# Retention and two MLPs on one core: two PSUM rings and a new order in the head, weight loads in quarters, and S3·T3 ahead of S1·T1 in the MLP pairs

## The chip, the cores and the metric

The kernel runs on one core of one Trainium2 chip. The metric is the time of one execution on the device in microseconds (us), lower is better. The kernel before takes 574.09 us, the median of three runs (573.87 to 574.21).

## The reference

Retention (a linear attention with decay) over 2 batches, 8 heads, 768 positions and head size 64, and then two MLPs on the 1536 tokens that it gives. The first MLP squares a ReLU, the second takes a leaky ReLU. q, k, v are float32, the weights are float64 and are converted on the chip.

```python
def _attn_ref(q, k, v, lam):
    Dmask = np.where(rel >= 0, lam[:, None, None] ** rel[None, :, :], 0.0)
    for b in range(nb):                      # blocks of positions
        intra = np.einsum('bhic,bhjc->bhij', qb, kb) * Dmask[None]
        intra = np.einsum('bhij,bhjd->bhid', intra, vb)
        inter = np.einsum('bhid,bhde->bhie', qb * lam_pow[None], kv_state)
        out[:, :, sl] = intra + inter
        kb_dec = kb * rev_pow[None]
        kv_state = lam_block[None, :, None, None] * kv_state + np.einsum('bhsd,bhse->bhde', kb_dec, vb)

def _moe_ref(x, w_in, w_out):                # x: 1536 x 512, d_ff 2048
    h = np.maximum(x @ w_in, 0.0)
    return (h * h @ w_out).astype(np.float32)

def _moe2_ref(x, w_in, w_out):
    h = x @ w_in
    g = np.maximum(0.01 * h, h)
    return (g @ w_out).astype(np.float32)
```

## The kernel before

**Precision.** Each operand of the MLPs is kept as a high and a low part (names with h and l), split by a cast on ACT and a subtraction on DVE (`split`, L68 to L70). A product is three matmuls: high by high, high by low, low by high. `three` (L523) issues them all from L525.

**Retention (the head).** The work goes in 12 units, i = 0 to 11: two batches of six chunks of 128 positions. For a unit, T(i) (`transposes`, L279) turns k and q on TensorE and ACT copies them out as kT and qT (L283); `scores` (L296) multiplies them into two PSUM banks; `mask` (L301, DVE) multiplies the scores by the decay table `DTr` into Pm; `state` takes k scaled by the decay (kd, L314, POOL), multiplies it with v (L320) and has DVE add the old state to it (`st`, L332, or L334 in the first chunk of a batch); the last chunk of a batch has no state. `output` (L345, L347) adds the state's part and Pm times v, and `split` makes xhi and xlo of the result. Every PSUM tile comes from one pool of eight banks in turn (`bank`, L59), the filler of `warm` included, and a tile takes its bank when the readers of the tile eight places before are done. `warm(n)` issues n transposes of the identity that nobody reads.

**Loads.** SP issues all loads in the order of the program: k and q four units ahead, v two units ahead, 256 KB each. Weights come in pieces of 1 MB (`fetch`, L92): two halves of the first MLP's first 512 columns, at i = 1 and i = 9, and the next behind retention. `converting` (L100) turns a piece from float64 into float32 in steps: on ACT `Abs` (L111), on DVE L112, L113, L115 and L118, then a cast to the high part on ACT (L132) and the low part on DVE (L134). During retention one step is placed in each of the units 3 to 7 (`convert(pin=True)`).

**The MLPs.** Each has four stages (l, s) of 512 columns of d_ff, and three token tiles of 512. From stage (0,1) on, tiles 0 and 1 are taken together in `first_pair`, a Strassen-like scheme of seven products in place of eight: A11·B11, S2·T2, A22·T4, S1·T1, S3·T3, A12·B21 and S4·B22, each for the halves h = 0, 1 of the columns. S1 to S4 are sums of weight blocks (`weight_sums`, L418; tiles `sw`, made by L423 to L426, a cast L427 and a subtraction L428), T1 to T4 sums of token blocks. PSUM tile A takes the A products, B takes S2·T2 and S3·T3, C takes S1·T1 and S4·B22, D takes A22·T4. `plus` (L595, DVE) adds them up, and `put` sends the finished block m = 2h + i of token tile t to `activate`: in layer 0 a ReLU, and its square twice, on ACT (L461 to L463), and the low part `g0l` or `g1l` on DVE (L467). Then `second(l, s, 0)` multiplies the blocks m = 0 to 3 of tile 0, in this order, by the second weight.

**What sets the order.** SP and TensorE run in the order of the program, in retention and, for TensorE, in the MLPs (`manual_schedule`). On ACT, DVE and POOL a scheduler sets the order at build time, by priorities: steps that are pinned (`keep_in_program_order`) keep their place, and `high_priority(offset=400)` in `put` and `plus` moves work forward. Each engine then runs its list in that order.

## Time and profile before

| what | before |
|---|---|
| median of three runs | 574.09 us (573.87 to 574.21) |
| the profiled execution's own time | 573.56 us |
| its span, first to last instruction | 571.6 us |
| TensorE (PE) busy | 561.2 us, 98% of the span |
| VectorE (DVE), ScalarE (ACT), GpSimd (POOL) busy | 71%, 53%, 16% |
| mean granted TensorE clock | 0.996 |
| first MLP matmul | 63.10 us from the span's start |

The profile is of one execution. Its page has the busy time of each engine, and views of the trace show single instructions in order of time, who waited for whom, the DMA issues with their time to landing, and the busy time in stretches that one chooses. The start of an instruction that had to wait carries the idle time ahead of it and what released it.

### The profile page before, as it was taken

How to read it: one execution, taken by the hardware profiler on the slowest of the kernel's cores; microseconds unless marked ns; L12 is line 12 of the kernel's file. 1: busy time of each engine (PE TensorE's matmuls, PEld its weight loads, DVE VectorE, ACT ScalarE, POOL GpSimd, SP SyncE). 2: the span in 40 equal slices, each digit the busy share in tenths (PEclk: the TensorE clock that was granted, in tenths of full speed). 3: DMA queues.
4: the chain of work that ended last, by engine and by line, in shares of the span. 5: the costliest groups of instructions: out<-in, count | busy, mean ns of one | idle time of the engine just before them, and what ended most of it. 6: DMA issues, size and time to landing. Idle time of an engine off the chain costs nothing.

```text
span 571.6 us, 8193 instructions
## 1 busy us (share of the span) xinstructions
PE 561.2 (98%) x3159; PEld 472.7 (83%) x3159; DVE 407.6 (71%) x595; ACT 304.6 (53%) x486; POOL 89.3 (16%) x101
## 2 busy tenths in 40 slices
PE   7999999999999999999999999999999999999997
PEld 7889888888788878888788888888888888888897
DVE  3588899999745584819888996719663492718887
ACT  2344589553974457733948555543662284435610
POOL 3659100000023202130000000000203101220032
PEclk9999999999999999999999999999999999999999
DMA  8998544535157744294413324354429505560444
GB/s 172 246 209 183 191 147 148 186 146 188 71 73 185 110 148 73 67 202 127 163 32 104 120 73 148 110 185 130 66 43 226 126 4 71 60 87 1 145 151 148
DMA packets 68472, 72.37 MB, mean 127 GB/s; under 512 B 39753, under 2 KB 43857, under 8 KB 68433
## 3 DMA queue, kind: packets, MB, share of 16 engines
...
q10 hardware_dynamic: 672, 0.39, 0.3%
q8 instruction: 25, 0.41, 0.3%
...
## 4 chain that ended last, share of the span: by engine, by line
PE 75%; DVE 11%; ACT 6%; DMA 4%; issue 2%; POOL 0%; SPq 0%; ACTq 0%; DVEq 0%; POOLq 0%
PE ps L525 67%; DMA raw<-in_moe_w_in 3%; DVE hb L118 2%; PE ps L279 2%; ACT f L461 2%; PE ps L296 2%; DMA raw<-in_moe_w_out 2%; PE ps L347 1%; DVE hb L115 1%; DVE f L595 1%; ACT g0h L462 1%; PE ps L345 1%; ACT hb L111 1%; ACT f L463 1%; PE ps L320 1%
## 5 line engine op out<-in xcount | busy, mean ns | idle before, releaser
L644 POOL DMA_DIRECT2D spill<-f x48 | 42.7, 918 | 408.3 <-ACT f L640 408.3
L525 PE MATMUL ps<-xhi,w1h 128*128 128x512 f32 x216 | 84.1, 390 | 0.0
L525 PE MATMUL ps<-xhi,w1l 128*128 128x512 f32 x216 | 84.0, 389 | 0.0
L525 PE MATMUL ps<-xlo,w1h 128*128 128x512 f32 x216 | 84.0, 389 | 0.0
L640 ACT COPY f<-ps 128x512 f32<-128x512 f32 x72 | 41.7, 584 | 70.3 <-PE ps L525 69.8
L134 DVE TENSOR_TENSOR w2l<-hb,w2h 128x1024 fp32r<-128x1024 f32 x16 | 19.6, 1227 | 61.1 <-ACT w2h L132 60.7
L467 DVE TENSOR_TENSOR g0l<-f,g0h 128x512 fp32r<-128x512 f32 x52 | 34.7, 686 | 34.2 <-ACT f L463 18.3
L595 DVE TENSOR_TENSOR f<-ps,f 128x512 f32<-128x512 f32 x70 | 45.7, 684 | 9.8 <-PE ps L525 9.3
L525 PEld LDWEIGHTS ps<-xhi,w1h 128*128 128x128 f32 x216 | 40.5, 188 | 8.5 <-issue 0.2
L525 PEld LDWEIGHTS ps<-xhi,w1l 128*128 128x128 f32 x216 | 40.5, 188 | 8.4
L525 PEld LDWEIGHTS ps<-xlo,w1h 128*128 128x128 f32 x216 | 40.5, 188 | 8.4
L525 PE MATMUL ps<-g0l,w2h 128*128 128x512 f32 x112 | 43.9, 392 | 3.0 <-DVE g0l L467 3.0
L111 ACT ACTIVATE hb<-raw 128x1024 f32<-128x1024 f32 x32 | 36.8, 1149 | 14.4 <-DMA raw<-in_moe_w_in 8.7
L118 DVE SCALAR_TENSOR_TENSOR hb<-raw,hb 128x1024 uint16<-128x1024 uint32 x32 | 43.6, 1364 | 0.4
L525 PE MATMUL ps<-g0h,w2l 128*128 128x512 f32 x112 | 43.6, 389 | 0.0
L525 PE MATMUL ps<-g0h,w2h 128*128 128x512 f32 x112 | 43.6, 389 | 0.0
L525 PE MATMUL ps<-t,sw 128*128 128x512 f32 x168 | 40.4, 389 | 0.0
L525 PE MATMUL ps<-w2l,g0h 128*128 128x512 f32 (+1 forms) x104 | 39.6, 381 | 0.0
L525 PE MATMUL ps<-w2h,g0l 128*128 128x512 f32 (+1 forms) x104 | 39.6, 381 | 0.0
L525 PE MATMUL ps<-w2h,g0h 128*128 128x512 f32 (+1 forms) x104 | 39.6, 381 | 0.0
L115 DVE SCALAR_TENSOR_TENSOR hb<-raw,hb 128x1024 uint32<-128x1024 uint32 x32 | 39.1, 1221 | 0.4
L525 PEld LDWEIGHTS ps<-t,sw 128*128 128x128 f32 x168 | 31.5, 188 | 6.5
...
## 6 DMA issues: line engine op xcount, KB each, us to landing
...
spill<-f POOLq DMA_DIRECT2D x48, 256.0 KB, 4.6
spill<-f SPq DMA_DIRECT2D x24, 256.0 KB, 3.1
k<-in_k SPq DMA_DIRECT2D x12, 256.0 KB, 4.7
q<-in_q SPq DMA_DIRECT2D x12, 256.0 KB, 5.0
v<-in_v SPq DMA_DIRECT2D x12, 256.0 KB, 5.3
f<-spill SPq DMA_DIRECT2D x12, 256.0 KB, 2.6
```

The costliest lines, as they stand in the source:

```text
L111: nc.scalar.activation(hf, w_hi.bitcast(F32), AF.Abs)
L115: yield ve.scalar_tensor_tensor(out=hb, in0=w_hi, scalar=0xC0000000, in1=hb, op0=ALU.bitwise_and, op1=ALU.bitwise_or)
L118: step = ve.scalar_tensor_tensor(out=half, in0=w_lo, scalar=2.0 ** -29, in1=half, op0=ALU.mult, op1=ALU.add)
L134: yield ve.tensor_tensor(out=lo, in0=hf, in1=hi, op=ALU.subtract)
L279: nc.tensor.transpose(ps[:, p, :], src[:, 2 * p:2 * p + 2, :].rearrange("s h d -> s (h d)"), ident)
L296: nc.tensor.matmul(raw_scores[i][par][:, p, :], kT[i][r, p, :], qT[i][r, p, :], start=True, stop=True)
L461: nc.scalar.activation(r, src, AF.Relu)
L467: nc.vector.tensor_tensor(out=glo, in0=r, in1=ghi, op=ALU.subtract)
L525: nc.tensor.matmul(ps, a, b, start=start and n == 0, stop=stop and n == len(ops) - 1, skip_group_check=again)
L595: ve.tensor_tensor(out=out, in0=ps[h, where], in1=other, op=ALU.add)
L640: nc.scalar.copy(f, src)
L644: nc.gpsimd.dma_start(dst, f, accum_op=ALU.add)
```

## The change

It has three parts. Line numbers shift by 7 in retention (L296 becomes L303), by 8 in `converting` (L111 becomes L119) and by 16 in the MLPs (L428 becomes L444, L467 becomes L483, L595 becomes L611).

1. **Head.** During retention PSUM is a pool of two rings of four banks: scores in one, everything else in the other. Behind `state(0)` come nine filler transposes, and T(2) stands ahead of `mask(0)` and `output(0)`. T(3) and `state(2)` stand behind `output(1)`, where T(3) stood ahead of it and `state(2)` behind T(4). For the MLPs a pool of eight banks in one ring is opened.
2. **Weights.** `fetch_by_rows` issues the two halves of the first weight as four loads of 256 KB each, one at each of the units 1 to 8; at i = 9 the first piece of the second weight follows. The conversion steps stand at the units 6 to 11. Later fetches hang on the conversion of the piece before.
3. **Pairs.** In `first_pair`, S3·T3 with its sums and the block m = 2h + 1 of tile 0 stands ahead of S1·T1. The sums per half are as many as before: r22 = B + s1, s1 = D + r22, and r22 + C once C is there.

```diff
@@ -54,10 +54,10 @@
     raw = ctx.enter_context(tc.tile_pool(name="raw", bufs=2))
     fp = ctx.enter_context(tc.tile_pool(name="fp", bufs=9))
     cv = ctx.enter_context(tc.tile_pool(name="cv", bufs=1))
-    psum = ctx.enter_context(tc.tile_pool(name="psum", bufs=8, space=bass.MemoryType.PSUM))
-
-    def bank():
-        return psum.tile([P, 512], F32, tag="ps", name="ps")
+    banks = []
+
+    def bank(tag="ps"):
+        return banks[-1].tile([P, 512], F32, tag=tag, name="ps")
 
     def plain():
         return fp.tile([P, TT], F32, tag="f", name="f")
@@ -89,6 +89,14 @@
     fetched, at_work = [], []
     wts, sums, opened = {}, {}, set()
 
+    def fetch_by_rows():
+        key = todo.pop(0)
+        r = raw.tile([P, 4 * CW], I64, tag="raw", name="raw")
+        fetched.append((key, r))
+        for k in range(4):
+            dma(r.rearrange("p (k f) -> p k f", k=4)[:, k], source(*key)[:, k])
+            yield
+
     def fetch():
         if todo:
             key = todo.pop(0)
@@ -116,7 +124,7 @@
                                       op0=ALU.bitwise_and, op1=ALU.bitwise_or)
 
         step = ve.scalar_tensor_tensor(out=half, in0=w_lo, scalar=2.0 ** -29, in1=half, op0=ALU.mult, op1=ALU.add)
-        if begun_mlp:
+        if key != order[0]:
             fetch()
         yield step
         if (l, s) != stages[0] and n == 0:
@@ -156,7 +164,6 @@
                 tc.keep_in_program_order(step)
 
 
-    begun_mlp = []
     opened.update(order[:5])
 
     xhi = [None] * NTILE
@@ -167,6 +174,7 @@
         xlo[t] = xp.tile([P, KD, TT], F32R, tag=f"xlo{t}", name=f"xlo{t}")
 
     def retention(ctx_att, att):
+        banks.append(ctx_att.enter_context(tc.tile_pool(name="early", bufs=4, space=bass.MemoryType.PSUM)))
         nat = {
             name: ctx_att.enter_context(tc.tile_pool(name="nat" + name, bufs=n))
             for name, n in (("k", 5), ("q", 3), ("v", 3))
@@ -198,9 +206,8 @@
         make_identity(nc, ident)
 
 
-        idle = bank()
-
         def warm(n):
+            idle = bank()
             for _ in range(n):
                 tc.keep_in_program_order(nc.tensor.transpose(idle[:, 0:P], ident, ident))
 
@@ -289,7 +296,7 @@
                 nc.gpsimd.tensor_tensor(out=qS[i], in0=qT[i], in1=LR, op=ALU.mult)
 
         def scores(i):
-            raw_scores[i] = [bank().rearrange("p (a s) -> p a s", a=NP) for _ in range(2)]
+            raw_scores[i] = [bank("scores").rearrange("p (a s) -> p a s", a=NP) for _ in range(2)]
             for p in range(NP):
                 for par in range(2):
                     r = slice(par * D, (par + 1) * D)
@@ -367,30 +374,38 @@
         scale_q(1, q1)
         scores(1)
         state(0)
+        warm(9)
+        q2 = transposes(2)
         mask(0)
         output(0)
-        scale_q(2, transposes(2))
+        scale_q(2, q2)
         state(1)
         mask(1)
         scores(2)
+        pieces = chain(fetch_by_rows(), fetch_by_rows())
         for i in range(n_units):
-            if i and i + 2 < n_units:
+            if i > 1 and i + 2 < n_units:
                 scale_q(i + 2, transposes(i + 2))
             if i + 4 < n_units:
                 load(i + 4, "kq")
             if i + 2 < n_units:
                 load(i + 2, "v")
-            if i in (1, 9):
+            if 1 <= i <= 8:
+                next(pieces)
+            if i == 9:
                 fetch()
             if i:
-                if i > 1:
+                if i > 2:
                     state(i)
                 output(i)
+                if i == 1:
+                    scale_q(3, transposes(3))
+                    state(2)
                 if i + 1 < n_units:
                     mask(i + 1)
                 if i + 2 < n_units:
                     scores(i + 2)
-            if 3 <= i <= 7:
+            if 6 <= i:
                 convert(pin=True)
 
 
@@ -398,7 +413,8 @@
         att = ctx_att.enter_context(tc.tile_pool(name="att", bufs=1))
         with tc.manual_schedule(engines={mybir.EngineType.SP, mybir.EngineType.PE}):
             retention(ctx_att, att)
-
+    banks.append(ctx.enter_context(
+        tc.tile_pool(name="psum", bufs=8, space=bass.MemoryType.PSUM, reuse_waits="tile")))
 
     late = ctx.enter_context(tc.tile_pool(name="late", bufs=1, reuse_waits="tile"))
     spill = [[[dram.tile([P, DM], F32, name=f"spill{l}{t}{m}") for m in range(4)] for t in range(NTILE)]
@@ -611,18 +627,18 @@
         if last:
             opened.add(("sums", l, s))
         for h in both:
+            product(h, "B", "S3", "T3", False)
+            r22[h] = plain()
+            plus(h, r22[h], "B", s1[h])
+            plus(h, s1[h], "D", r22[h])
+            put(h, s1[h], s1[h], 1, 0)
+            yield last
+        for h in both:
             product(h, "C", "S1", "T1")
+            plus(h, r22[h], "C", r22[h])
             yield True
         for h in both:
-            product(h, "B", "S3", "T3", False)
-            plus(h, s1[h], "B", s1[h])
-            r22[h] = plain()
-            plus(h, r22[h], "C", s1[h])
-            plus(h, s1[h], "D", s1[h])
-            yield last
-        for h in both:
             put(h, product(h, "A", "A12", "B21", False), plain(), 0, 0)
-            put(h, s1[h], s1[h], 1, 0)
             yield last
         for h in both:
             product(h, "C", "S4", "B22", False)
@@ -792,8 +808,6 @@
             return parts + [first(l, s, 2)] + [second_last(s, t) for t in range(NTILE)]
         return parts + [second(l, s, 0), first(l, s, 2), second(l, s, 1), second(l, s, 2)]
 
-    begun_mlp.append(True)
-    fetch()
     opened.update(order[:7])
     with tc.manual_schedule(engines={mybir.EngineType.PE}):
         for l, s in stages:
```

How the compiled order of the instructions changes is shown at three places, on the engines whose order the scheduler sets; TensorE's and SP's order is that of the code above. A row is a line of the program, the operation, the tile written and the tiles read.

**DVE, in stage (0,1), from the conversion of a weight piece to the sums of the pair.** `hb_1663` (after, `hb_1678`) is the piece, L595 (L611) the `plus` sums. Before:

```order
L113 TENSOR_SCALAR hb_1663<-hb_1663 128x1024
L115 SCALAR_TENSOR_TENSOR hb_1663<-raw_1562,hb_1663 128x1024
L118 SCALAR_TENSOR_TENSOR hb_1663<-raw_1562,hb_1663 128x1024
L595 TENSOR_TENSOR f_1608<-ps_1623,f_1608 128x512
L595 TENSOR_TENSOR f_1689<-ps_1666,f_1608 128x512
L595 TENSOR_TENSOR f_1618<-ps_1636,f_1618 128x512
```

After:

```order
L121 TENSOR_SCALAR hb_1678<-hb_1678 128x1024
L611 TENSOR_TENSOR f_1695<-ps_1649,f_1631 128x512
L123 SCALAR_TENSOR_TENSOR hb_1678<-raw_1577,hb_1678 128x1024
L611 TENSOR_TENSOR f_1631<-ps_1671,f_1695 128x512
L611 TENSOR_TENSOR f_1708<-ps_1660,f_1643 128x512
L611 TENSOR_TENSOR f_1695<-ps_1715,f_1695 128x512
```

Both of the piece's long steps stood ahead of the six sums. Now the first of them (L123) stands between the sum r22 = B + s1 of half 0 and the sum s1 = D + r22 made from it, and the second comes after the sums.

**DVE, in stage (0,1), ahead of `second(l, s, 0)`.** `g0l` are the low parts of tile 0's blocks, L428 (after, L444) is the subtraction for `sw`. Before:

```order
L467 TENSOR_TENSOR g0l_1598<-f_1608,g0h_1597 128x512
L595 TENSOR_TENSOR f_1630<-ps_1666,f_1630 128x512
L595 TENSOR_TENSOR f_1643<-ps_1674,f_1643 128x512
L467 TENSOR_TENSOR g0l_1598<-f_1723,g0h_1597 128x512
L467 TENSOR_TENSOR g0l_1598<-f_1618,g0h_1597 128x512
L428 TENSOR_TENSOR sw_1633<-rb_1632,sw_1633 128x1024
```

After:

```order
L483 TENSOR_TENSOR g0l_1621<-f_1643,g0h_1620 128x512
L611 TENSOR_TENSOR f_1656<-ps_1715,f_1656 128x512
L483 TENSOR_TENSOR g0l_1621<-f_1741,g0h_1620 128x512
L611 TENSOR_TENSOR f_1667<-ps_1724,f_1667 128x512
L444 TENSOR_TENSOR sw_1646<-rb_1645,sw_1646 128x1024
L483 TENSOR_TENSOR g0l_1621<-f_1752,g0h_1620 128x512
```

The third block's low part, `g0l_1598<-f_1723` before and `g0l_1621<-f_1752` after, stood ahead of the subtraction for `sw` and right behind the two last sums. Now the last sum and the subtraction stand in front of it.

**ACT, at the end of retention.** L283 (after, L290) are the copies kT and qT, L69 the high part of an output, L111 (L119) a conversion's `Abs`, L140 the cast of a converted piece; the two rows `xhi2` in each list are those of units 9 and 10. Before:

```order
L283 COPY kT_865<-ps_860 128x512
L283 COPY qT_872<-ps_867 128x512
L69 CAST xhi2_843<-ps_896 128x4x128
L111 ACTIVATE hb_1033<-raw_878 128x1024
L69 CAST xhi2_843<-ps_944 128x4x128
```

After:

```order
L290 COPY kT_880<-ps_875 128x512
L290 COPY qT_887<-ps_882 128x512
L119 ACTIVATE hb_1005<-raw_636 128x1024
L140 CAST w1h0_982<-hb_730 128x1024
L69 CAST xhi2_857<-ps_911 128x4x128
L69 CAST xhi2_857<-ps_960 128x4x128
```

Between the copy qT and `xhi2` of unit 9 now stand the `Abs` of the second weight half (`raw_636`) and the cast of the first (`w1h0`). The `Abs` that stood between the two `xhi2` is gone.

## Rows read from the trace of the kernel before

**Rows 1.** The page: span, and busy time (share) of TensorE.

```profile
span 571.6 us, 8193 instructions
...
PE 561.2 (98%) x3159; PEld 472.7 (83%) x3159; DVE 407.6 (71%) x595; ACT 304.6 (53%) x486; POOL 89.3 (16%) x101
```

**Rows 2.** Table of waits: who waits for whom, us in total, times, longest.

```profile
PE ps L525 <- DVE g0l L467: 3.0, 3, 1.0
```

**Rows 3.** Timeline of TensorE, head: start us, duration us, instruction, count, [idle before <-releaser].

```profile
13.94 1.12 PE L320 MATMUL ps<-v,kd 128*64 128x64 f32 x16 [1.70 <-issue]
...
18.75 1.16 PE L296 MATMUL ps<-qT,kT 64*128 64x128 f32 x16 [0.17 <-ACT qT L283]
...
22.77 1.16 PE L296 MATMUL ps<-qT,kT 64*128 64x128 f32 x16
...
25.40 0.39 PE L345 MATMUL ps<-qS,st 128*64 128x128 f32 x4
...
32.21 1.16 PE L296 MATMUL ps<-qT,kT 64*128 64x128 f32 x16 [0.41 <-ACT qT L283]
```

**Rows 4.** Stretches: us, each engine's busy us, granted clock, DMA share, GB/s.

```profile
14.00:15.00 1.00, 1.00 (x18) 1.00 (x20) 1.00 (x3) 0.00 (x0) 0.09 (x1) 0.50 1.34 229
```

**Rows 5.** Timeline of ACT around unit 4.

```profile
30.03 1.18 ACT L111 ACTIVATE hb<-raw 128x1024 f32<-128x1024 f32 x1 [2.08 <-DMA raw<-in_moe_w_in]
```

**Rows 6.** Timelines of TensorE, ACT and DVE in stage (0,1).

```profile
147.56 0.39 PE L525 MATMUL ps<-g0h,w2h 128*128 128x512 f32 x1
...
148.92 0.39 PE L525 MATMUL ps<-g0h,w2h 128*128 128x512 f32 x1
150.25 0.50 PE L525 MATMUL ps<-g0l,w2h 128*128 128x512 f32 x1 [0.94 <-DVE g0l L467]
...
143.73 0.58 ACT L461 ACTIVATE f<-ps 128x512 f32<-128x512 f32 x1
...
149.89 1.04 ACT L427 CAST sw<-rb 128x1024 fp32r<-128x1024 f32 x1
...
138.60 1.23 DVE L115 SCALAR_TENSOR_TENSOR hb<-raw,hb 128x1024 uint32<-128x1024 uint32 x1
```

**Rows 7.** Timeline of TensorE in stage (0,2).

```profile
212.70 0.39 PE L525 MATMUL ps<-g0h,w2h 128*128 128x512 f32 x1
214.09 0.51 PE L525 MATMUL ps<-g0l,w2h 128*128 128x512 f32 x1 [1.01 <-DVE g0l L467]
```

**Rows 8.** Timeline of SP's DMA issues.

```profile
8.82 0.73 SPq L66 DMA_DIRECT2D q<-in_q  x1
...
16.95 1.06 SPq L66 DMA_DIRECT2D q<-in_q  x1
18.06 0.85 SPq L66 DMA_DIRECT2D v<-in_v  x1
19.01 0.97 SPq L66 DMA_DIRECT2D k<-in_k  x1
...
47.19 2.10 SPq L66 DMA_DIRECT2D v<-in_v  x2
```

**Rows 9.** DMA issues at 8.82, 16.95, 19.01: count, KB, us to landing.

```profile
q<-in_q SPq DMA_DIRECT2D x1, 256.0 KB, 6.8
...
q<-in_q SPq DMA_DIRECT2D x1, 256.0 KB, 4.3
...
k<-in_k SPq DMA_DIRECT2D x1, 256.0 KB, 4.6
```

**Rows 10.** Timelines of ACT, DVE and TensorE, end of retention.

```profile
57.86 0.58 ACT L69 CAST xhi<-ps 128x512 fp32r<-128x512 f32 x1 [1.68 <-PE ps L347]
...
60.28 0.87 DVE L332 TENSOR_TENSOR st<-ps,tmp 64x256 f32<-64x256 f32 x2
...
61.10 0.43 PE L345 MATMUL ps<-qS,st 128*64 128x128 f32 x3
...
63.10 0.50 PE L525 MATMUL ps<-xhi,w1h 128*128 128x512 f32 x1
```

2 lines of the change are left out of this document (1 added, 1 removed).

## The prediction

> **What bounds the kernel now.** The page's engine list comes first: TensorE is busy for 561.2 of 571.6 us [rows 1], so the time moves only by what TensorE waits for, and by the clock it is granted. The table of waits then says where. The only wait of its matmuls in the two MLPs is for DVE's `g0l`, the low part of an activation, three times [rows 2]; the rest lies in the first 33 us. There TensorE's timeline shows `state(0)` starting at 13.94 after 1.70 us of idle time [rows 3]: the eight-bank ring hands it a bank with raw scores in it, which `mask(0)` has yet to read. In the us after this the granted clock is 0.50, the 1.2 GHz level [rows 4]. A smaller hole, 0.41 us, stands ahead of scores(5) at 32.21 [rows 3]: ACT took the weight conversion's `Abs` (L111, 1.18 us from 30.03) ahead of the copies of kT and qT [rows 5].
>
> The three MLP holes stand at one place, in stages (0,1), (0,2) and (0,3): in `second(l, s, 0)`, where the third block of activations, m2, is first used. In (0,1) it starts at 147.56, goes six steps of 0.227 us to 148.92, and the next matmul starts at 150.25 [rows 6]; (0,2) shows the same with 212.70 and 214.09 [rows 7], and (0,3) like it. Call E the start of `second`, 147.56 in (0,1) and 212.70 − 6 × 0.227 = 211.34 in (0,2). The matmul that waits starts at E + 2.69 in the one and at E + 2.75 in the other (2.79 in the third), where E + 1.59 would be its own pace. So each stage loses 1.1 to 1.2 us, and the matmul that restarts another 0.1: 3.8 us in all.
>
> **Part 1, the head.** With score tiles in a ring of their own, `state(0)` no longer waits for DVE. Nine filler transposes and T(2), the transposes of unit 2, come ahead of output(0), so `mask(0)` has some 3 us of cover. What ends last afterwards is a load, twice. T(2) needs q2, issued at 8.82 [rows 8] and landed 6.8 us later [rows 9], at 15.6; then output(0) and state(1) follow (some 2 us), so scores(2) starts at 17.6, against 18.75 [rows 3]. From scores(2) to scores(3), TensorE took 4.0 us before (22.77 − 18.75, with T(3) and output(1) between) [rows 3]; the same work now ends at about 21.5. There `state(2)` stands, moved ahead of scores(3) and T(4), and it needs v2. SP issues that at 18.06, between q4 (16.95) and k5 (19.01) [rows 8]; those took 4.3 and 4.6 us to land [rows 9], so 21.25 and 23.6. SP's order up to there is unchanged, and I take their middle, 22.4, as an estimate for v2. TensorE thus waits about 0.9 us, and then owes state(2), scores(3) and T(4), which took 25.40 − 22.77 = 2.63 us before [rows 3]: output(2) starts at 22.45 + 2.63 = 25.08 against 25.40, −0.32. Bounds: if v2 lands with q4, −1.25; if with k5, +0.9.
>
> The clock is the other unknown. After the filler TensorE idles about 0.8 us for k2 and 0.5 us for q2, where it idled 1.70 in one piece. If it is granted 0.50 again for some 3 us, T(2), output(0) and state(1) take up to 1.7 us longer, but 0.9 of that disappears in the wait for v2. I count 0, with 0.8 as the bound, since the idle pieces are shorter than the one in the row.
>
> **Part 2, weight quarters and later conversion steps.** The same bytes go out as quarter loads behind units 1 to 8, so no 1 MB load stands between v3 and k6 any more. The first conversion step comes at unit 6 and not 3, which removes the hole ahead of scores(5), 0.48 us with its restart. The head is thus 0.80 us early from there on. What the moved steps cost lies at the end of retention. Before, ACT idles 1.68 us ahead of xhi9 at 57.86, so from 56.18, where its copy of qT(11) ends [rows 10]. Now the compiled order has the `Abs` of the second weight half and the cast of the first there, L119 and L140. At −0.80 the copy ends at 55.38 and `Abs` at 56.5; the cast, which also needs DVE's last conversion step (to about 56.35), ends at 57.55. So xhi9, which TensorE would allow at 57.06, starts at 57.55. Behind it come xlo9, mask(11) and the `st` of state(10), which ends 60.28 + 0.87 − 57.86 = 3.29 us after xhi9's start [rows 10], so at 60.84. Output(11) could start at 61.10 − 0.80 = 60.30, needs `st` between 60.4 and 60.84, and the first MLP matmul follows 2.00 us behind its start (63.10 − 61.10) [rows 10], at 62.4 to 62.85. I take 62.8, near the late end, since the second half of `st` is needed within its first matmuls: **−0.3 us** for the head as a whole (bounds −1.6 and +0.9).
>
> **Part 3, S3·T3 ahead of S1·T1.** The number of products and of DVE adds is the same. What changes is when each ends: B is complete one pair of products (12 matmuls, 2.7 us) earlier, so blocks m1 and m3 can leave early, and C's add comes later. What it may bring can be read from the hole: ACT did twelve activations back to back from 143.73 to the cast at 149.89, 0.51 us each [rows 6], and m2 was the last of them. Moving m1 ahead takes three from that line, 1.5 us. But the compiled order puts something else in front of m2: on ACT the cast for `sw` (1.04 us), and on DVE the last add of S4 and the subtraction for `sw` (L428 before, L444 now; as long as L115, 1.23 us [rows 6]). In the old order both stood behind m2.
>
> Walk of (0,2) and (0,3): m2's relu starts on ACT near E − 0.7, the cast ends near E + 0.35, m2's two squares at E + 1.9. DVE does the last add when S4 is done, E + 0.3 to E + 1.0, then the subtraction to E + 2.15, then `g0l` of m2 to E + 2.85. TensorE restarts at E + 2.8 to 2.9, against 2.75 to 2.79 before. I take +0.06 each; bounds −0.4, where the squares bind alone, and +0.2.
>
> Walk of (0,1): here a weight conversion is under way. Before, its L115 (138.60, 1.23 us) stood ahead of all these adds [rows 6]; now it stands between the first add, at 138.6, and the second, which makes m1's input. So that input is ready at 141.13. ACT starts then, waits for DVE's adds until 142.9, and reaches the relu of m0 at 144.94 instead of 143.73; m0's second square ends at 147.64, and the first matmul with `g0l`, due at E + 0.23, waits until E + 0.83. That is a new hole of 0.6 us, ahead of the old one. The cast ends at 149.1, the subtraction at 150.36, m2's `g0l` at 150.97, and TensorE restarts at 151.03 instead of 150.25: **+0.78**. Bounds +0.2 and +1.2. The second MLP has no such holes, as the three of the table are all in the first [rows 2], and there m2's `g0l` stays ahead of the subtraction: 0.
>
> **Sum.** −0.3 + 0.78 + 2 × 0.06 = +0.6 us. The profiled execution took 573.56 us, 2.0 more than its span [rows 1]; with +0.6 it would take 574.2. The median of the runs shown, 574.09, is 0.53 above it, and the sum on top of that gives **574.7 us**. A measurement of this kernel can tell about 0.2%, or 1.15 us, from no change, so this counts as the same.
>
> **Rivals.**
> A. The MLP holes close, if m2's `g0l` is not held by the subtraction. For it: ACT, which bound before, is relieved of three activations. Against it: the fixed order on DVE. All three closed give 574.09 − 3.8 − 0.3 = 570.0; one or two closed give 571 to 573.
>
> B. The head keeps 0.8 us or more (v2 early, `st` in time) and (0,1) loses little: 572.6 to 573.4.
>
> C. Slower: a quarter lands late and holds ACT in front of xhi9. ACT runs in order, so an `Abs` that waits for the eighth quarter blocks xhi9, mask(11) and output(11); this decides from 55.4 us on. The quarter goes out behind the last v load there, whose issue ended at 49.3 before [rows 8], so near 48.5; at 4.3 to 4.8 us to land it is there by 53.3, 2 us early. Each us beyond 55.4 is a us at the end: a landing at 57 gives 576.3. The Trainium skill, DMA: Bandwidth & Descriptors, section Anatomy of one DMA, speaks for this rival: it counts a fixed cost of about 2.0 us for each DMA besides its bytes (a fit for GpSimd's path); with six DMAs more, paid one after the other, that is 12 us of queue time, an estimate by that page, and the eighth quarter would be late. The rows of this queue speak against adding them up: q4 and k5 were issued 2.06 us apart and landed 2.35 us apart with a load between, though each took over 4 [rows 8, 9].
>
> D. Slower: all three stages go like (0,1): 3 × 0.78 − 0.3 = +2.0, 576.1.
>
> E. Slower: rings of four bring back waits on banks. An output now takes the bank of the output before it and waits for that unit's xlo, with some 1.2 us of margin at full pace; a delay of ACT's xhi beyond that, up to 0.8 us at unit 6, goes to the end: 575.5. The Trainium skill, Perfetto Trace Analysis, section Matmul Optimizations, asks that all eight banks be in use; by that rule the narrow rings cost. The row of `state(0)` shows the wide ring costing 1.70 us [rows 3].
>
> **How the numbers follow.** Forecast 0.50 (573.6 to 575.2 by its bounds), A 0.10 whole and 0.08 in part, B 0.08, C 0.10, D 0.08, E 0.06. Faster by over 0.2% (under 572.9): A and half of B, 0.22. Slower by over 0.2% (over 575.2): C, D, E and the edge of the forecast, 0.28. Same: 0.50. The range of 8 in 10 runs from A in part to C and D, 570.7 to 576.6; it leaves out A whole and landings later than 57.
>
> **What would show it.** No idle time ahead of `state(0)`, and a wait at `state(2)` for v2 of 0.5 to 1.3 us; scores(5) near 31.4 without a hole; xhi9 behind a cast, and the first MLP matmul at 62.4 to 62.9. In (0,1) two waits for `g0l`, at E + 0.2 and at m2, restart near E + 3.5; in (0,2) and (0,3) one wait, restart at E + 2.8. If the table of waits shows no `g0l`, rival A holds and my walk of DVE's order is wrong; a granted clock of 0.50 past 17 us, or an `Abs` that waits for a load near 55, breaks the head's term.

## The result, and the profile after

The changed kernel takes 577.99 us (median of 4 runs, 576.84 to 578.95), against 574.15 us for the kernel before in the same comparison (573.87 to 574.57): a ratio of 1.0066, interval 1.0049 to 1.0083. It is slower by 0.7%, outside the predicted range of 570.7 to 576.6. The profiled execution took 578.04 us with a span of 576.3, so the trace has 4.7 us more than that of before [rows 1] to account for.

The page of after, busy times, and its table of waits (who waits for whom, us in total, times, longest):

```profile
PE 563.6 (98%) x3168; PEld 473.8 (82%) x3168; DVE 406.7 (71%) x595; ACT 306.6 (53%) x486; POOL 89.4 (16%) x101
```

```profile
PE ps L541 <- DVE g0l L483: 3.4, 4, 1.2
PE ps L352 <- DVE st L339: 1.8, 1, 1.8
```

The wait for `g0l` grew from 3.0 to 3.4 us and from three to four times [rows 2]. New is one wait of 1.8 us, for `st`. TensorE's timeline of after shows it ahead of output(11) and, 3.19 us behind its start, the first MLP matmuls (start us, duration, instruction, count, [idle before <-releaser]):

```profile
14.41 0.63 PE L286 MATMUL ps<-ident,k 128*128 128x128 f32 x4 [0.65 <-DMA k<-in_k]
15.54 0.63 PE L286 MATMUL ps<-ident,q 128*128 128x128 f32 x4 [0.49 <-DMA q<-in_q]
...
22.84 0.69 PE L327 MATMUL ps<-v,kd 128*64 128x64 f32 x16 [1.01 <-DMA v<-in_v]
...
63.04 0.78 PE L352 MATMUL ps<-qS,st 128*64 128x128 f32 x3 [1.85 <-DVE st L339]
...
66.23 0.80 PE L541 MATMUL ps<-xhi,w1h 128*128 128x512 f32 x1
66.82 0.63 PE L541 MATMUL ps<-xlo,w1h 128*128 128x512 f32 x1
```

ACT and DVE of after at the end of retention, same columns, show what `st` stood behind:

```profile
58.16 1.17 ACT L119 ACTIVATE hb<-raw 128x1024 f32<-128x1024 f32 x1 [2.07 <-DMA raw<-in_moe_w_in]
59.24 1.03 ACT L140 CAST w1h<-hb 128x1024 fp32r<-128x1024 f32 x1
60.17 0.57 ACT L69 CAST xhi<-ps 128x512 fp32r<-128x512 f32 x1
```

```profile
60.77 0.69 DVE L70 TENSOR_TENSOR xlo<-ps,xhi 128x512 fp32r<-128x512 f32 x1 [2.53 <-ACT xhi L69]
61.38 1.28 DVE L308 TENSOR_TENSOR Pm<-ps,DTr 128x512 f32<-128x512 f32 x2
62.58 0.86 DVE L339 TENSOR_TENSOR st<-ps,tmp 64x256 f32<-64x256 f32 x2
```

`Abs` waits 2.07 us for the eighth quarter, and xhi9, mask(11) and `st` stand in line behind it: xhi9 starts at 60.17, before at 57.86 [rows 10]. Then the clock falls. Stretches of 1 us of after (us, busy us of PE, PEld, DVE, ACT, POOL, granted clock, DMA share, GB/s):

```profile
63.00:64.00 1.00, 0.94 (x12) 0.70 (x14) 0.96 (x2) 0.00 (x0) 0.00 (x0) 1.00 0.00 0
64.00:65.00 1.00, 1.00 (x18) 1.00 (x16) 0.97 (x2) 0.22 (x1) 0.00 (x0) 0.72 0.00 0
65.00:66.00 1.00, 1.00 (x12) 0.90 (x8) 0.47 (x2) 0.92 (x1) 0.00 (x0) 0.50 0.07 16
...
68.00:69.00 1.00, 1.00 (x6) 0.83 (x5) 1.00 (x2) 0.00 (x0) 0.00 (x0) 1.00 0.00 0
```

Output(11) takes 66.23 − 63.04 = 3.19 us in place of 2.00 [rows 10], and the first MLP matmuls lose 0.75 us more at 0.50, the 1.2 GHz level. Not all of the 1.19 is the clock: in x1, x3 and v6 below output(11) takes 2.24 to 2.35 us at a clock of 1.00, so 0.84 to 0.95 us is. The rest is lost in its first matmuls, probably while the second half of `st` is still being made. The MLPs' holes in after:

```profile
151.98 0.50 PE L541 MATMUL ps<-g0l,w2h 128*128 128x512 f32 x1 [0.15 <-DVE g0l L483]
...
154.57 0.50 PE L541 MATMUL ps<-g0l,w2h 128*128 128x512 f32 x1 [0.92 <-DVE g0l L483]
```

```profile
218.59 0.50 PE L541 MATMUL ps<-g0l,w2h 128*128 128x512 f32 x1 [1.17 <-DVE g0l L483]
```

From here on, "holes" is the time between starts of MLP matmuls beyond their pace of 0.227 us, restarts included, summed over the trace without gaps of under 0.02 us: 3.9 us before. A hole is named by the start of the matmul ahead of it. By it stage (0,1) went from 1.21 to 1.61 us, (0,2) and (0,3) from 1.3 to 1.45 each. So the 4.7 us are 3.13 (first MLP matmul at 66.23, before at 63.10), 0.75 (clock) and 0.7 (pairs' holes); 0.1 lies behind the last of these matmuls.

### The profile page after: what moved, and what is told of

Its sections match the earlier page's. It is cut to its first block, busy times and chain, and to the rows that moved or that the text cites. A ratio compares the mean times of both kernels' runs of the same rounds, so it can differ in the third digit from the quotient of the medians.

```text
span 576.3 us, 8246 instructions
## 1 busy us (share of the span) xinstructions
PE 563.6 (98%) x3168; PEld 473.8 (82%) x3168; DVE 406.7 (71%) x595; ACT 306.6 (53%) x486; POOL 89.4 (16%) x101
## 4 chain that ended last, share of the span: by engine, by line
PE 84%; DVE 6%; ACT 3%; DMA 3%; issue 2%; SPq 0%; DVEq 0%; ACTq 0%
PE ps L541 78%; DVE f L611 2%; PE ps L286 1%; PE ps L354 1%; PE ps L303 1%; ACT f L477 1%; PE ps L352 1%; DMA q<-in_q 1%; ACT g0h L478 1%; DMA v<-in_v 1%; DMA raw<-in_moe_w_in 1%; DVE g0l L483 1%; PE ps L327 1%; DVE sw L444 1%; DVE hb L126 0%
## 5 line engine op out<-in xcount | busy, mean ns | idle before, releaser
L142 DVE TENSOR_TENSOR w2l<-hb,w2h 128x1024 fp32r<-128x1024 f32 x16 | 19.7, 1228 | 60.8 <-ACT w2h L140 60.4
L483 DVE TENSOR_TENSOR g0l<-f,g0h 128x512 fp32r<-128x512 f32 x52 | 35.5, 690 | 35.6 <-ACT f L479 18.8
L611 DVE TENSOR_TENSOR f<-ps,f 128x512 f32<-128x512 f32 x70 | 46.0, 689 | 6.4 <-PE ps L541 6.3
L119 ACT ACTIVATE hb<-raw 128x1024 f32<-128x1024 f32 x32 | 36.7, 1147 | 17.1 <-DMA raw<-in_moe_w_in 6.4
L123 DVE SCALAR_TENSOR_TENSOR hb<-raw,hb 128x1024 uint32<-128x1024 uint32 x32 | 39.1, 1222 | 0.5
```

The costliest lines, as they stand in the source:

```text
L119: nc.scalar.activation(hf, w_hi.bitcast(F32), AF.Abs)
L123: yield ve.scalar_tensor_tensor(out=hb, in0=w_hi, scalar=0xC0000000, in1=hb, op0=ALU.bitwise_and, op1=ALU.bitwise_or)
L142: yield ve.tensor_tensor(out=lo, in0=hf, in1=hi, op=ALU.subtract)
L483: nc.vector.tensor_tensor(out=glo, in0=r, in1=ghi, op=ALU.subtract)
L611: ve.tensor_tensor(out=out, in0=ps[h, where], in1=other, op=ALU.add)
```

## The experiments

Theory 1 after the result was rival C: the hold on ACT and the clock fall behind it are the loss. Its rival: that other parts of the change cost by themselves. Times are medians; each ratio is to the kernel before in the same comparison, and the last two columns are of the profiled execution, which for x3, y1, w3 and v5 is the shortest of their four.

| run | us (range) | ratio (interval) | first MLP matmul | holes, us |
|---|---|---|---|---|
| before | 574.15 (573.87–574.57) | | 63.10 | 3.9 |
| the change | 577.99 (576.84–578.95) | 1.0066 (1.0049–1.0083) | 66.23 | 5.4, 0.86 of it clock |
| x1 `Abs` in order | 577.30 (575.81–578.22) | 1.0056 (1.0040–1.0071) | 64.09 | 6.2 |
| x2 pairs only | 575.09 (574.10–576.07) | 1.0019 (1.0010–1.0027) | 63.22 | 4.7 |
| x3 all but the pairs | 578.47 (576.57–580.02) | 1.0074 (1.0056–1.0093) | 64.35 | 5.7 |
| x4 filler at the end | 578.91 (576.70–581.28) | 1.0084 (1.0060–1.0108) | 65.89 | 7.1 |
| y1 rings only | 577.02 (575.85–577.72) | 1.0047 (1.0032–1.0062) | 63.99 | 5.5 |
| y2 quarters only | 577.44 (576.50–577.79) | 1.0052 (1.0036–1.0067) | 65.51 | 5.2 |
| y4 one half in quarters | 576.89 (576.81–580.10) | 1.0060 (1.0037–1.0084) | 64.41 | 6.1 |
| z1 pairs, weight steps later | 572.85 (572.05–574.84) | 0.9981 (0.9971–0.9991) | 63.51 | 2.7 |
| w1 rings, state(2) back | 575.24 (574.54–577.21) | 1.0024 (1.0012–1.0035) | 63.06 | 5.5 |
| w2 second pool only | 575.20 (574.06–577.15) | 1.0020 (1.0008–1.0032) | 63.91 | 5.3 |
| w3 half the bytes | 576.64 (575.90–577.35) | 1.0043 (1.0028–1.0058) | 63.23 | 6.1 |
| z2 z1, steps at 4 to 8 | 572.86 (572.25–573.96) | 0.9980 (0.9970–0.9989) | 63.61 | 2.7 |
| v3 w1 in one pool | 574.37 (573.41–576.87) | 1.0016 (1.0002–1.0029) | 63.41 | 4.0 |
| v4 v3 and z1's pairs | 572.96 (571.64–574.14) | 0.9982 (0.9970–0.9994) | 63.70 | 2.7 |
| v5 x1 in one pool | 577.93 (576.95–578.44) | 1.0071 (1.0055–1.0088) | 63.88 | 6.5 |
| v6 y2, `Abs` in order | 578.17 (575.14–578.54) | 1.0064 (1.0042–1.0087) | 65.01 | 6.6 |
| u1 steps at unit 6 only | 575.72 (575.08–576.13) | 1.0023 (1.0011–1.0035) | 63.47 | 5.2 |

### The hold alone: x1, x4, x3, x2

x1 is the changed kernel with the head's `Abs` kept in program order:

```diff
-        nc.scalar.activation(hf, w_hi.bitcast(F32), AF.Abs)
+        absolute = nc.scalar.activation(hf, w_hi.bitcast(F32), AF.Abs)
+        if pin:
+            tc.keep_in_program_order(absolute)
```

> The changed kernel with one thing undone: the conversion's Abs keeps its place on ACT behind the output split that the program has ahead of it, so the Abs of the second weight half, which waits for the eighth quarter (landed about 57.7 us), stands behind xhi9 to xhi11 and not ahead of xhi9. Theory 1 (the late quarter held ACT, through it xhi9, mask(11), the state and output(11), and the idle TensorE then lost its full clock): output(11) starts at 61.0 and not 63.04, no wait of TensorE for st, granted clock 1.00 through the start of the MLP, first MLP matmul near 62.9 to 63.1, and the time falls by 3.9 us to about 574.1 (573.8 to 575.0). Theory 2 (the two rings, the filler and the new order of transposes cost the time themselves): no change, 577 to 578.

The wait for `st` and the clock fall are gone and the first block begins at 64.09, but the time fell by 0.7 us only, and not by 3.9; the two intervals overlap. State(9) waits 0.96 us for v9 at 51.65, and stage (0,1) has a hole of 1.50 us at 148.86 that after does not have. Nor was the hold all that x1 changed. TensorE and POOL have the order of the change, but on DVE 23 rows and on ACT 37, from 41 to 131 us, stand elsewhere: pinning one instruction moved others. So the hold is real, and it is not the whole loss, but x1 does not give its price by itself.

x4 puts 15 filler transposes ahead of output(11):

```diff
                     state(i)
+                if i == n_units - 1:
+                    warm(15)
                 output(i)
```

> The changed kernel with fifteen filler transposes (15 x 0.11 = 1.6 us) on TensorE between output(10) and output(11), where it waits 1.85 us for the state. The wait itself stays: output(11) at 63.0. If the clock of 0.50 from 64.3 to 67.4 comes from that idle time, it stays at 1.00, output(11) takes 2.0 us and not 3.2, the first MLP matmul comes at 65.0 and runs at 0.227 us at once: minus 1.9 to 2.0 us, about 576.0. If it comes from something else (the light load of the small matmuls of the whole head), the clock still falls and the time stays at 577 to 578.

The clock stayed at 1.00 from 60 to 69 us, and the time did not fall. The hold is still there (`Abs` at 58.64), so the first block began at 65.89, and a hole of 2.31 us stood at 100.70, where TensorE waits for a low part (`t`) on DVE. There two conversion steps stand ahead of it:

```profile
100.23 1.22 DVE L142 TENSOR_TENSOR w1l<-hb,w1h 128x1024 fp32r<-128x1024 f32 x1
101.36 1.22 DVE L123 SCALAR_TENSOR_TENSOR hb<-raw,hb 128x1024 uint32<-128x1024 uint32 x1
102.50 0.69 DVE L485 TENSOR_TENSOR t<-f,t 128x512 fp32r<-128x512 f32 x1
```

In after only the first of the two stands between the last two such low parts. The filler takes a bank, and with it 26 rows on DVE and 34 on ACT, from 67 to 130 us, stand elsewhere than in the change. So x4 shows that the clock can be held, and not what that is worth.

x3 is the changed kernel with the old `first_pair`, x2 the kernel before with the new one (the diff's last part):

```diff
+            product(h, "B", "S3", "T3", False)
...
+            put(h, s1[h], s1[h], 1, 0)
...
             product(h, "C", "S1", "T1")
```

> The changed kernel with the old order in the pairs: head and quarters alone. Theory 1: the whole loss of 3.1 us at the first MLP matmul and 0.75 us of slow matmuls behind it stay, the MLP holes are those of before (1.21, 1.29, 1.31 us): 577.0 to 577.5, that is 0.7 below the changed kernel. Rival (the pairs' order is the larger part): under 576.

> The kernel before with only S3.T3 and its sums ahead of S1.T1 in the pairs. Theory (DVE's subtraction for sw now stands ahead of the third low part, and one conversion step between two sums): the three holes of TensorE at second(l, s, 0) stay and grow by 0.4 in stage (0,1) and by 0.15 in (0,2) and (0,3), 0.7 us in all, 574.6 to 575.0. Rival (the reordering closes the holes when the head is not disturbed): minus 1 to 3.8, 570.3 to 573.1.

x2 costs 0.9 us with 0.74 us more of holes and the head of before: the pairs' part went as forecast, 0.1 us above its range. x3 is as slow as the whole change, so the head and the weights lose it; it missed both of its ranges (578.47). In its trace, of the shortest of its four runs, the eighth quarter was issued at 52.28 and landed 4.1 us later, so `Abs` did not wait:

```profile
57.00 1.21 ACT L119 ACTIVATE hb<-raw 128x1024 f32<-128x1024 f32 x1
```

The first block began at 64.35 at a clock of 1.00, and this run took 576.57 us. So the hold comes in some executions and not in others, and without it, and without the new pairs, the change is still 2.4 us slower than before.

### The head's parts: y1, y2, y4

y1 has the rings, the filler and the order of T and state(2), with the loads and conversion steps of before; y2 has only the quarters and the later steps; y4 has the changed head with one half in quarters and the second as one load of 1 MB at i = 9. Both y1 and y4 have the old pairs.

```diff
 y1
-            if 1 <= i <= 8:
-                next(pieces)
-            if i == 9:
+            if i in (1, 9):
                 fetch()
...
-            if 6 <= i:
+            if 3 <= i <= 7:
```

```diff
 y4
-        pieces = chain(fetch_by_rows(), fetch_by_rows())
+        pieces = fetch_by_rows()
...
-            if 1 <= i <= 8:
+            if 1 <= i <= 4:
...
-            if 6 <= i:
+            if 6 <= i <= 10:
```

y2 is the other side of y1: those lines of the change put into the kernel before.

> The kernel before with the head's first part alone: the two rings, the nine filler transposes, T(2) ahead of output(0), T(3) and state(2) behind output(1). Loads and conversion steps as before (1 MB at units 1 and 9, steps at 3 to 7), pairs as before. Theory 1 (the loss comes from the quarters: the queue carries 1 MB more by unit 8): no loss here, first MLP matmul at 62.6 to 63.2, 573.5 to 574.3. Theory 2 (rings and order cost by themselves): 576 to 577.

> The kernel before with the weight part alone: eight quarter loads at units 1 to 8, the next piece at 9, conversion steps at units 6 to 11. One ring of eight banks, old order of transposes, old pairs. Theory 1 (the quarters fill the queue that brings k, q and v, so the last quarter lands near 57 to 58 and holds ACT ahead of xhi9): first MLP matmul at 64 to 66, 576 to 578, with a wider spread between runs than the kernel before. Theory 2 (rings and order): 574.

> The changed head with only the first weight half in quarters, at units 1 to 4; the second half is one load of 1 MB at unit 9, as before; conversion steps at units 6 to 10; old pairs. Theory 1 (what costs is the second MB in the queue by unit 8, not the quarters as such): no late Abs ahead of xhi9, no late v, first MLP matmul at 62.3 to 63.0, 573.3 to 574.2. If quarter loads cost by their number, half of the loss stays: 575.5 to 576.5.

y1, expected level by its theory 1, is 2.6 us slower: the theory that this part is harmless fell. TensorE waits 1.2 us for v2 at 23.0, and holes of 0.87 and 1.49 us stand at 98.8 and 150.8. y2 is 3.0 us slower, within its theory 1. Its ACT, at unit 6, shows rival C's hold a second time, at the fourth quarter:

```profile
43.36 1.12 ACT L119 ACTIVATE hb<-raw 128x1024 f32<-128x1024 f32 x1 [2.69 <-DMA raw<-in_moe_w_in]
...
44.85 0.59 ACT L290 COPY qT<-ps 128x512 f32<-128x512 f32 x1
```

TensorE's scores wait 1.9 us there for qT. y4 has the same hold (0.9 us ahead of output(6)) and holes of 1.60 and 1.29 us at 99.3 and 152.0, and at 576.89 us it is above both of its ranges. So leaving the second half as one load does not mend it; as y4 keeps y1's head and the late steps, it does not price the quarters.

### What makes y1 slow: w1, w2, v3

w1 is y1 with `state(2)` back behind T(4):

```diff
                 if i == 1:
                     scale_q(3, transposes(3))
-                    state(2)
...
-                if i > 2:
+                if i > 1:
                     state(i)
```

> Rings, filler and unit 3's transposes ahead of state(2), with the loads, conversions and pair order of before, as in the run with the rings alone, but state(2) goes back behind unit 4's transposes, where before has it. The run with the rings alone waited 1.2 us for v2 at 23.0 us and 0.8 us for qT5 at 33.0 us, and its first block began at 63.99 us. Theory 1 (the early state(2) asks for v2 before it is there, and the filler's 0.5 us is not hidden): the wait for v2 is under 0.3 us, the first block begins at 62.6 to 63.0 us and the time is 574.0 to 575.7 us, by whether the two holes near 98.8 and 150.8 us stay (1.5 us together over before). Theory 2 (the loads set the pace of these units, whatever order asks for them): the wait comes back in another row, the first block begins at 63.8 us or later and the time is 576.5 to 577.2 us.

The wait for v2 fell to 0.2 us, the first block came 0.93 us earlier, and the holes stayed: 575.24 us, within theory 1.

w2 is the kernel before with one edit, a pool of eight banks for retention and a second one of eight for the MLPs:

```diff
+        banks.append(ctx_att.enter_context(tc.tile_pool(name="early", bufs=8, space=bass.MemoryType.PSUM)))
...
+    banks.append(ctx.enter_context(
+        tc.tile_pool(name="psum", bufs=8, space=bass.MemoryType.PSUM, reuse_waits="tile")))
```

> The kernel before with one edit: the retention has a pool of eight banks of its own, and the later stages get a second pool of eight banks that waits by tile, as in the changed kernel; order, loads and conversions are those of before. Theory 1 (the second pool costs nothing; the holes near 98.8 and 150.8 us in the runs of the changed head come from when its conversions ran): first block at 63.1 us, holes as before (148.9, 212.7, 276.6 us, 3.9 us in all), 574.2 us within 0.4. Theory 2 (the pool holds the first block, or the banks handed out in another order make the holes): first block at 63.4 us or later, or a hole of 0.5 us or more near 98.8 us; 574.8 to 575.8 us.

It is 1.2 us slower, within theory 2, with holes of 0.88 us at 98.7 and 1.49 at 150.8, though TensorE's instructions stand in the order of before, one by one. DVE's do not. DVE in the first blocks, before and then w2:

```profile
69.00 1.22 DVE L134 TENSOR_TENSOR w1l<-hb,w1h 128x1024 fp32r<-128x1024 f32 x1
70.13 0.68 DVE L467 TENSOR_TENSOR g0l<-f,g0h 128x512 fp32r<-128x512 f32 x1
70.73 1.39 DVE L118 SCALAR_TENSOR_TENSOR hb<-raw,hb 128x1024 uint16<-128x1024 uint32 x1
```

```profile
69.86 1.22 DVE L134 TENSOR_TENSOR w1l<-hb,w1h 128x1024 fp32r<-128x1024 f32 x1
71.00 1.36 DVE L118 SCALAR_TENSOR_TENSOR hb<-raw,hb 128x1024 uint16<-128x1024 uint32 x1
72.22 0.70 DVE L470 TENSOR_TENSOR g0l<-f,g0h 128x512 fp32r<-128x512 f32 x1
```

A conversion step stands ahead of a block's `g0l`, and the low parts stay behind from there on, until TensorE waits for one at 98.7:

```profile
99.84 0.50 PE L528 MATMUL ps<-t,w2h 128*128 128x512 f32 x1 [0.71 <-DVE t L470]
```

The later first block of this trace (63.91) is another matter: TensorE waits 1.58 us for qT at 33.02, in the head, where no engine's order differs from before.

v3 is w1 with both rings in one pool, which the MLPs go on using by turns:

```diff
+    psum = ctx.enter_context(tc.tile_pool(name="psum", bufs=4, space=bass.MemoryType.PSUM))
...
-    banks.append(ctx.enter_context(
-        tc.tile_pool(name="psum", bufs=8, space=bass.MemoryType.PSUM, reuse_waits="tile")))
+    turn += ["ps", "scores"]
```

> The run with rings, filler and unit 3's transposes, state(2) put back (575.24 us; first block at 63.06 us; holes at 97.9 and 149.9 us, 5.5 us of them in all), with one edit: the two rings lie in one pool of 2 x 4 banks that the later stages go on using by turns, so no second pool is opened. TensorE's order is unchanged by that; on DVE and ACT 49 and 45 rows of the first blocks stand elsewhere, which are then those of before. Theory 1 (the second pool costs by the order that it gives the conversions among the first blocks' own steps): no hole near 98 us, about 1.1 us near 149 us, 3.9 us in all, first block at 63.0 to 63.3 us, 573.7 to 574.3 us, level with before. Theory 2 (the holes come from the rings or the filler): they stay, 575.2 us.

The table of waits of v3:

```profile
PE ps L540 <- DVE g0l L482: 3.0, 3, 1.0
```

That is the row of before [rows 2]. DVE and ACT have the order of before in the MLPs again, the holes of w1 are gone, and the time is 574.37, 0.07 above theory 1's range, a ratio of 1.0016 whose interval just leaves out 1. By their times alone w1 and v3 are not told apart (their intervals overlap); by their holes, 5.5 and 4.0 us, they are. So y1's loss is `state(2)` (1.3 us, from y1 to w1) and the second pool; rings and filler gain nothing.

### What makes y2 slow: w3, v6, v5, u1

w3 is the changed kernel with each quarter carrying half of its columns; DVE zeroes the rest at the start:

```diff
-            dma(r.rearrange("p (k f) -> p k f", k=4)[:, k], source(*key)[:, k])
+            dma(r.rearrange("p (k f) -> p k f", k=4)[:, k, 0:CW // 2], source(*key)[:, k, 0:CW // 2])
...
```

> The changed kernel, with each of the eight quarters carrying half of its columns (0.125 MB in place of 0.25); the other half of these two weight blocks is set to zero by DVE at the start of the program, so half of the first two weight blocks is left out of the sums. Nothing else moves. Theory 1 (the queue is full from 8 us on, so the eighth quarter is issued 4 us later than its step and holds Abs on ACT): it is issued by 49.5 us and lands by 54 us, ACT does not stand idle in front of xhi9, output(11) begins by 61.5 us, the first block begins at 62.8 to 63.9 us, and the time is 574.6 to 576.0 us (the pairs' 0.7 us stays). Theory 2 (not the bytes, but the count of transfers on SP or the place of the conversions): the eighth quarter is still issued after 51.5 us, the first block begins after 65 us, 577 us or more.

SP of the changed kernel, and then of w3, from the load of v9 on; the last row of each is the eighth quarter:

```profile
48.24 3.27 SPq L66 DMA_DIRECT2D v<-in_v  x1
51.57 0.77 SPq L66 DMA_DIRECT2D raw<-in_moe_w_in  x1
52.43 0.38 SPq L66 DMA_DIRECT2D v<-in_v  x1
52.87 0.57 SPq L66 DMA_DIRECT2D raw<-in_moe_w_in  x1
```

```profile
46.44 1.42 SPq L66 DMA_DIRECT2D v<-in_v  x1
47.91 1.12 SPq L66 DMA_DIRECT2D raw<-in_moe_w_in  x1
49.13 0.39 SPq L66 DMA_DIRECT2D v<-in_v  x1
49.56 1.78 SPq L66 DMA_DIRECT2D raw<-in_moe_w_in  x1
```

It goes out 3.3 us earlier, `Abs` starts at 54.34, xhi9 is not held and the first block begins at 63.23: the bytes make the landing late. Before, the second half went out only behind all of this; and in both kernels the queue was busy from 22 to 53 us (before and then after; the last two columns are DMA share and GB/s):

```profile
53.80 0.57 SPq L66 DMA_DIRECT2D raw<-in_moe_w_in  x1
```

```profile
22.00:53.00 31.00, 30.59 (x486) 27.30 (x484) 24.23 (x38) 13.51 (x23) 20.92 (x21) 1.00 1.02 217
```

```profile
22.00:53.00 31.00, 30.16 (x472) 26.99 (x472) 20.07 (x35) 12.54 (x23) 19.70 (x20) 1.00 1.05 222
```

Yet w3's time missed its range by 0.6 us. The hole of 1.50 us in stage (0,1) stands here too (at 148.02). Every engine has the order of the change here, but for the fills on DVE at the start and this `Abs`, which stands ahead of the copies of kT(11) and qT(11). So the changed kernel does not show the hole because its first block begins 3 us later.

v6 is y2 with x1's edit, v5 is x1 with v3's single pool.

```diff
 v6
+        if pin:
+            tc.keep_in_program_order(absolute)
```

```diff
 v5
-        tc.tile_pool(name="psum", bufs=8, space=bass.MemoryType.PSUM, reuse_waits="tile")))
+    turn += ["ps", "scores"]
```

> The run with the quarters alone (577.44 us; scores waits 1.9 us at 45.5 us for qT, which stands behind Abs on ACT while Abs waits for the fourth quarter; two waits of 0.8 us together near 63 us; first block at 65.51 us), with Abs kept in program order. Theory 1 (the hold on ACT is the quarters' cost in the head): the wait at 45.5 us falls under 0.4 us, the first block begins at 62.8 to 63.6 us, and the time is 574.8 to 575.8 us, the holes near 150 us remaining. Theory 2 (the quarters delay k, q and v themselves): waits for k, q or v of over 1 us in all come in their place, the first block begins after 64.3 us, 576.3 us or more.

> The changed kernel with Abs in program order (577.3 us; first block at 64.09 us, a hole of 1.50 us at 148.9 us beside the pairs' own), and in one pool as above. Theory 1 (the pool's order of conversions makes that hole): the hole falls under 0.5 us, 575.6 to 576.4 us. Theory 2 (the quarters make it: the first blocks' conversions run late because the loads behind the quarters land late): the hole stays over 1 us, 577 us or more.

v6 has no wait at 45.5 us, as theory 1 wanted, but output(11) waits 1.1 us for `st` and the first block begins at 65.01. Neither theory gave that. DVE and then ACT of v6 show the hold in another instruction:

```profile
56.48 2.31 DVE L128 SCALAR_TENSOR_TENSOR hb<-raw,hb 128x1024 uint16<-128x1024 uint32 x1
```

```profile
44.91 1.17 ACT L119 ACTIVATE hb<-raw 128x1024 f32<-128x1024 f32 x1
...
58.83 1.05 ACT L142 CAST w1h<-hb 128x1024 fp32r<-128x1024 f32 x1 [2.64 <-DVE hb L128]
59.78 0.58 ACT L69 CAST xhi<-ps 128x512 fp32r<-128x512 f32 x1
```

The cast is that of the first half. It waits for this half's last conversion step on DVE, and xhi9 stands behind it as it stood behind `Abs`. No load is in this chain: the first half's `Abs` ran at 44.91 without a wait. Its steps come one per unit from unit 6 on, the last one at unit 10, and that one took 2.31 us here, 1.36 in w3. So the late steps can hold xhi9 too, without a late load. v5, at 577.93 us within theory 2, keeps its hole of 1.50 us at 149.0: with the quarters and the late steps, the pool is not what makes it.

u1 is the kernel before with the steps three units later:

```diff
-            if 3 <= i <= 7:
+            if 6 <= i:
                 convert(pin=True)
```

> The kernel before with one edit: the conversion steps of the head begin at unit 6 and not at unit 3, as in the changed kernel; loads, pool, rings and pairs are those of before. Every run of the changed head's quarters has a hole of 1.3 to 1.6 us near 99 or 150 us, also without the second pool. Theory 1 (the steps' late start makes it: DVE has some 5 us of the first weights' conversion left to do when the first blocks begin): holes of 5.2 us or more in all, against 3.9; first block at 62.7 to 63.4 us; 575.0 to 576.0 us. Theory 2 (the quarters' late landing makes it): holes of 3.9 us in all, first block at 62.7 to 63.2 us, 573.7 to 574.3 us.

It is 1.4 us slower, within theory 1, with loads, pool and rings of before. TensorE in stage (0,1) of u1:

```profile
148.82 0.50 PE L525 MATMUL ps<-g0l,w2h 128*128 128x512 f32 x1 [0.50 <-DVE g0l L467]
...
151.90 0.50 PE L525 MATMUL ps<-g0l,w2h 128*128 128x512 f32 x1 [1.27 <-DVE g0l L467]
```

These are y2's holes (0.7 and 1.5 us with the restarts). Why DVE cannot take the steps later shows in its busy time, in stretches (PE, PEld, DVE, ACT, POOL), before and then u1:

```profile
28.00:43.00 15.00, 14.59 (x222) 12.85 (x220) 12.66 (x19) 6.39 (x11) 7.93 (x8) 1.00 1.03 212
...
63.00:143.00 80.00, 80.00 (x355) 66.18 (x353) 77.40 (x103) 53.54 (x79) 0.00 (x0) 1.00 0.48 159
```

```profile
28.00:43.00 15.00, 13.96 (x210) 12.34 (x211) 8.36 (x16) 6.28 (x11) 6.43 (x7) 1.00 1.03 211
```

DVE does 4.3 us less between 28 and 43 us, and from 63 to 143 us it is busy for 77 of 80 us in both: what the head leaves undone is not made up before stage (0,1).

### A version that beats both: z1, z2, v4

z1 is the kernel before with the new pairs (not shown again), and the cast and subtraction for `sw` (L427, L428) kept behind the pair's blocks:

```diff
+        while pairing:
+            yield None
+        hold = tc.keep_in_program_order
+        hold(nc.scalar.copy(both[:, 0], f))
+        yield hold(ve.tensor_tensor(out=both[:, 1], in0=f, in1=both[:, 0], op=ALU.subtract))
```

z2 adds `4 <= i <= 8` for the conversion steps, v4 is v3 with z1's pairs.

```diff
 z2
-            if 3 <= i <= 7:
+            if 4 <= i <= 8:
```

```diff
 v4
+        psum = ctx.enter_context(tc.tile_pool(name="psum", bufs=4, space=bass.MemoryType.PSUM))
...
+            put(h, s1[h], s1[h], 1, 0)
...
+        while pairing:
+            yield None
```

> The kernel before with the new order in the pairs, and with the cast and the subtraction for sw kept behind the pair's blocks on ACT and DVE, so that the third low part stands directly behind the last sum. Theory (that subtraction in front of the third low part is what holds TensorE in (0,2) and (0,3)): the third matmul at E + 2.2 and not E + 2.9 there, holes of 0.6 to 0.7 us and not 1.45; in (0,1) the hole ahead stays (0.3 to 0.4) and the second shrinks from 1.08 to 0.7. In all 2.0 us below the pair order alone, 573.1 (572.6 to 573.8). Rival (ACT binds and the subtraction only seems to): no change against the pair order alone, 575.1.

> The kernel before with the pairs' new order and the weight sums' last two steps behind the pair's blocks (572.85 us when it ran), and the five conversion steps in the head one unit later (units 4 to 8). Theory 1 (Abs of the first block holds qT5 on ACT at 30 us while its weights land; moved on, it holds nothing): the gap near 32 us falls from 0.7 to 1.7 us to about 0.2, the first block begins at 62.5 to 63.0 us, 572.1 to 572.5 us. Theory 2 (the conversions are then late for the first blocks, as in the runs with the late half): first block at 63.1 us or later, or a hole near 100 us; 572.8 to 574.0 us.

> The kernel of the run before this one, with the pairs' new order and the weight sums' last two steps behind the pair's blocks (572.85 us on top of the head of before). If what each part is worth adds: 572.5 to 573.0 us, holes of 2.7 us in all, first block at 63.0 to 63.3 us. If the rings and the filler are worth something once the pool and state(2) are set right: 572.4 us or less. If they still cost: 573.3 us or more.

z1's wait for `g0l`:

```profile
PE ps L529 <- DVE g0l L470: 1.6, 3, 0.7
```

It is half of before's 3.0 [rows 2], and the time is 572.85 us, 0.2% under before and, by the two ratios, some 5 us under the change. z1 and v4 lie in the ranges forecast. z2 and v4 come out level with z1; z2's time is in theory 2's range, but its trace does not show that theory's late conversions. z2's gap at 32 us fell to 0.33 us, but a wait of 2.2 us at state(0), put down to POOL's `qS`, stood in that trace and the first block began no earlier (63.61). The rings are again worth nothing.

## Why the prediction was wrong

The head's term, −0.3 us in the sum, is what failed. In it the landing of the eighth quarter was wrong, and two costs stood at nothing.

- **The head up to unit 10** went nearly as put. State(0)'s wait is gone, v2 holds TensorE 1.01 us at 22.84 (put: 0.9 at 22.45), scores(5) has no hole, and the clock stays at 1.00 from 13 to 17 us. But the gain is smaller: scores(5) starts at 31.95 against 32.21 [rows 3], where 31.4 was put, and output(10) at 59.27 against 59.35, 0.08 us early and not 0.80. Part 1 was put at −0.32 by the start of output(2), which came at 25.57, 0.17 late; moving `state(2)`, which is part of it, costs 1.3 us by y1 and w1.
- **The eighth quarter** is the step that failed in Part 2, and rival C, which had a chance of 0.10, came true. It was expected to go out near 48.5 us and to land by 53.3; it went out at 52.87 and landed at 57.7. I read the issue time from the row of v's load before [rows 8] and took the bytes of this stretch as the same. But before, only one of the two halves is loaded between 22 and 53 us; the second goes out at 53.8. The change asks for both there, with a queue that was busy in both kernels (DMA share 1.02 and 1.05), so the loads behind came later. The rival's own price holds: `Abs` would have been harmless until 55.4 us, so 57.7 is 2.3 us late, and output(11) starts at 63.04, 2.2 to 2.6 us behind the 60.4 to 60.84 put. The sign named for it came too: an `Abs` that waits for a load near 55 (2.07 us, to 58.16). w3 has as many transfers and half of the quarters' bytes, and 3.3 of the 4.4 us went away, so most of it is bytes. With the bytes of before in this stretch, w3 has issued v10 by 49.5, against 49.3 before [rows 8]. The Trainium skill, DMA: Bandwidth & Descriptors, section Anatomy of one DMA, counts a fixed cost of about 2.0 us for each DMA besides its bytes (a fit for GpSimd's path); added up over the six DMAs more, that is not what w3 shows.
- **The clock behind the wait** was not in the sum or in a bound: 0.84 to 0.95 us in output(11) and 0.75 in the first MLP matmuls. The text had a fall of the clock only for the head's start (0.8 as a bound, and as a sign past 17 us).
- **Part 3** was right in sum: 0.78 + 2 × 0.06 = 0.9 put, 0.7 us of holes in after and in x2, 0.9 us in x2's time. The split was off: 0.4 in (0,1) and 0.15 in each of the others, so that the sum came out is in part luck. The walk's cause, the `sw` subtraction in front of `g0l`, is borne out by z1, which moves it, and its cast on ACT with it, and gains 2.2 us over x2.
- **Two costs stood at nothing.** The second pool stood in the diff and had no price. By itself it costs 1.2 us (w2), by the order that the scheduler gives DVE and ACT. And the moved conversion steps were priced only where they land, at the end of retention, not for the room on DVE that they leave unused at 28 to 43 us: 1.4 us by themselves (u1). Halving the quarters' bytes gave back 1.3 of the change's 3.8 us by the ratios (w3), so these two weigh at least as much as the late landing.
- **Rival E** did not come true: with the second pool gone, v3 is within 0.16% of before. The two rings together use all eight banks.
- **The parts do not add.** Pairs 0.9, rings 2.6 and quarters 3.0 make 6.5 us; the change costs 3.8. The late first block hides the hole in (0,1) that w3 shows once it comes earlier, and x1 and v5 show one of the same size. Taken out one behind the other, they lead back: 1.0066 for the change, 1.0074 without the new pairs (x3), 1.0047 without the quarters and late steps too (y1), 1.0024 with `state(2)` put back (w1), 1.0016 without the second pool (v3). Neighbours' intervals overlap or nearly do, so the sizes of these steps are rough.

Open: what the hold and the clock are worth with all else in place, since x1 and x4 moved other instructions as well; how the quarters' own cost beyond u1 (y2's 1.0052 against 1.0023, some 1.7 us) divides between the two holds; and how much of the runs' wider spread with the changed head (2.1 us, before 0.7) is the landing of its loads, where x3's trace shows a run without the hold.
